# Reordering the load queue of a fused SSM and gated-MLP kernel: one x block forward, one small transpose and one row back

## The chip, the cores and the metric

The kernel runs on one core of one Trainium2 chip. The metric is the device time of one execution in microseconds. Six runs of the kernel before gave a median of 177.17 us, from 176.81 to 177.47.

## What is computed

The input x is 2048 tokens by 512 features. It is layer-normalised, and three results are added: x itself, a diagonal complex state-space layer (S5) with a skip term, and a gated MLP.

```
xn = layernorm(x)
# A: state space, P = 512 complex states
dt = exp(log_dt);  Lam_bar = exp(dt * Lambda)
Bu = xn @ B_bar.T                 # B_bar = (Lam_bar - 1) / Lambda * (B_re + i B_im)
h[t] = Lam_bar * h[t-1] + Bu[t]   # 2048 steps
yA = 2 * Re(h @ C.T) + xn * Dskip
# B: gated MLP, F = 1376
yB = (gelu(xn @ w_gate) * (xn @ w_up)) @ w_down
out = x + yA + yB
```

## The kernel before

**Tiling.** The 2048 tokens are four blocks (0 to 3) of 512 tokens; each block is four tiles of 128 tokens. `X` holds the raw tiles, `XN` the normalised ones (a ring of eight tiles), and `XNT[b]` the normalised block with features on the partitions, as TensorE needs it. A "turn" is a DMA transpose that takes one normalised tile from `XN` to `XNT` (`TR`, L736, four per block).

**Stages on TensorE (PE), in program order.** First a warm-up, then block 0's first seven gate and up column groups by another route: raw centred tiles are transposed on PE (`cent_T`, L679) and multiplied with the weights (`ks`/`GT_k` at L701, `GT_mm` at L712), and the scale of the layernorm goes into the GELU afterwards (`GT_evac`, L721 and L724). This stage needs no turn. Then `GU(0, [7, 8, 9, 10])` (L843, and L817 for the last, narrower group) does the rest of block 0's gate and up columns from `XNT[0]`; every one of its matmuls waits for all four turns of block 0. `BU(0)` and `BU(1)` (L749) multiply `XNT[0]` and `XNT[1]` by the state-space input matrices `BBT`; the first two units of `BU(1)` are halved, so that they can begin with the first two turns of block 1. After that come `GU(1)`, `BU(2)`, the down projection `DN(0)` (L884) and so on to `DN(3)`.

**VectorE (DVE), ScalarE (ACT) and GpSimd (POOL).** DVE does the layernorm statistics (`stats`, L610 and L611), the normalisation (`norms`, L629), the product of GELU and up (L724, L864), the sine tables (`tables_dve`, L597 and L599), the skip product (`SKIP`, L666) and the scan along the tokens (`CHAIN`). ACT does the GELUs and the copies out of the accumulators. POOL computes powers: the square roots of the layernorms (`root`, L617) and two exponentials of the state-space parameters (`params`, L552 for exp(log_dt), L555).

**What sets the order.** A list scheduler inside the kernel (`Sched`) places the operations of DVE, ACT and POOL by a cost model. TensorE and SyncE (SP) are in its list `INORDER`: their instructions stay in the order in which the program names them. Almost all DMAs are issued by SP, so a line's place in the program is its place in SP's queue, and an instruction of SP that waits holds up all those behind it. Up to block 1's turns SP issues, in this order:

```
x tiles of block 0 (one of them on ACT's queue), gate/up weights in pieces     L493, L484, L489
the last gate and up pieces (480 KB each), load_W                              L489
tr_par: the small transpose of log_dt, Lambda_re, Lambda_im                    L510
TR(0): four turns of block 0                                                   L736
ld_x(1): x of block 1, 512 KB                                                  L478
load_B: transposes of B_re and B_im                                            L521
        D-skip row, broadcast to 128 partitions, 128 KB                        L530
        ld_x(2): x of block 2, 512 KB                                          L478
TR(1): four turns of block 1                                                   L736
then the turns of the gated rest (L829), of block 0's hidden tiles (L730), TR(2), ...
```

The parameters of `tr_par` are read first by `params` (POOL L552, then DVE L553 and L556); the D-skip row is read first by `SKIP(0)` (L666); x of block 1 by `LN(1)` (`stats`, `root`, `norms`).

Of the kernel before, what the change touches and what calls it, by code (L numbers as in the profile page):

```python
# [352 lines left out]
def d_dve_tt2x(n): return 100.0 + 0.52 * n  # L353
# [4 lines left out]
def d_act(n, ptr=0): return 190.0 + 0.833 * n + 90.0 * ptr  # L358
# [3 lines left out]
def build(nc, ins, out):  # L362
    with ExitStack() as es:
# [113 lines left out]
        def ld_x(b):  # L477
            return S.dma(lambda e, b=b: e.dma_start(  # L478
                X_all.ap[:, 4 * b:4 * b + 4, :], x2[512 * b:512 * (b + 1), :].rearrange("(j p) d -> p j d", p=128)),
                512 * 1024, writes=X[4 * b:4 * b + 4], tag="ld_x%d" % b)  # L480
# [28 lines left out]
        def tr_par():  # L509
            S.dma(lambda e: e.dma_start_transpose(PAR.ap.rearrange("p q t -> p (q t)").unsqueeze(1), PROW16.ap), 4096,  # L510
                  reads=PROWq, writes=[PAR], tag="tr_par", issue=900.0)
# [7 lines left out]
        def load_T(bufs, nms):  # L519
            for b_, nm in zip(bufs, nms):  # L520
                S.dma(lambda e, b_=b_, nm=nm: e.dma_start_transpose(b_.ap, ins[nm]),  # L521
                      1.4 * 512 * 1024, writes=[b_], tag="tr_" + nm, issue=3000.0)

        def load_W():
            ld_w(WG, WGc, ins["B_w_gate"], 2)
            ld_w(WU, WUc, ins["B_w_up"], 2)

        def load_B():
            load_T([A.sub(BBT_all, "BBTc%d" % c, c) for c in range(2)], ("A_B_re", "A_B_im"))
            S.dma(lambda e: e.dma_start(DSKB.ap, ins["A_Dskip"].unsqueeze(0).broadcast_to([128, D])),  # L530
                  128 * 1024, writes=[DSKB], tag="ld_dsk")
            ld_x(2)

        def load_C():
            load_T(CRAW, ("A_C_re", "A_C_im"))
# [15 lines left out]
        def params():  # L551
            S.order_behind(POOL(lambda e: e.tensor_tensor(DTB.ap, EXB.ap, LDT.ap, ALU.pow), 1100, [EXB, LDT], [DTB], "exp_dt"), GATE["pow"])  # L552
            V(lambda e: e.tensor_tensor(pa(TH), DTB.ap, LIM.ap, ALU.mult), D_TINY, [DTB, LIM], [PA[TH]], "th")  # L553
            V(lambda e: e.tensor_tensor(pa(A_), DTB.ap, LRE.ap, ALU.mult), D_TINY, [DTB, LRE], [PA[A_]], "a")
            POOL(lambda e: e.tensor_tensor(pa(RRr), EXB.ap, pa(A_), ALU.pow), 1100, [EXB, PA[A_]], [PA[RRr]], "exp_a")  # L555
            V(lambda e: e.tensor_scalar(w16(0, 4), pa(TH), 1.0 / TWO_PI, None, ALU.mult), D_TINY, [PA[TH]], [W16p[0]])  # L556
            V(lambda e: e.tensor_scalar(w16(4, 8), pa(TH), 512.0 / TWO_PI, None, ALU.mult), D_TINY, [PA[TH]], [W16p[1]])
            V(lambda e: e.tensor_scalar(w16(8, 16), w16(0, 8), 0.25, None, ALU.add), D_TINY, W16p[0:2], W16p[2:4])
            V(lambda e: e.tensor_copy(KI.ap, W16.ap), D_TINY, W16p, [KI])
            V(lambda e: e.tensor_tensor(FRC.ap, W16.ap, KI.ap, ALU.subtract), D_TINY, W16p + [KI], [FRC])  # L560
# [34 lines left out]
        def tables_dve(behind):  # L595
            for s in range(KP):
                V(lambda e, s=s: e.tensor_scalar(K1s[s].ap, IOTJ.ap, W16.ap[:, s:s + 1], None, ALU.mult),  # L597
                  d_dve_ts4x(512) * 1.3, [IOTJ, W16p[0]], [K1s[s]], "k1", [GATE["evTA"]])
                V(lambda e, s=s: e.scalar_tensor_tensor(F1s[s].ap, IOTJ.ap, W16.ap[:, s:s + 1], K1s[s].ap, ALU.mult, ALU.subtract),  # L599
                  d_dve_1x(512), [IOTJ, W16p[0], K1s[s]], [F1s[s]], "f1")  # L600
            S.order_behind(V(lambda e: e.tensor_scalar(A1.ap.bitcast(I32), F1.ap.bitcast(I32), 0x7FFFFFFF, None, ALU.bitwise_and), d_dve_ts4x(2048) * 2, F1s, [A1], "a1"), behind)
# [6 lines left out]
        def stats(b, j):  # L608
            tt = 4 * b + j
            return (V(lambda e: e.bn_stats(ST[tt].ap, X[tt].ap), d_dve_1x(512), [X[tt]], [ST[tt]], "bnst"),  # L610
                    V(lambda e: e.bn_aggr(MVt[b][j].ap, ST[tt].ap), D_TINY, [ST[tt]], [MVt[b][j]], "bnag"))  # L611

        def root(b, j0, j1):
            mn, sbq, qb, rq = (cols(t, b, j0, j1) for t in (MN, SBQ, QB, RQ))
            mv = Buf("MV%d_%d_%d" % (b, j0, j1), "sb", MVt[b][j0].lo, MVt[b][j1 - 1].hi, MV[b].ap[:, j0:j1])
            op = V(lambda e: e.tensor_scalar(sbq.ap, mv.ap[:, :, 1], EPS_BF16, None, ALU.add), D_TINY, [mv], [sbq], "sbq")
            GATE["pow"] = POOL(lambda e: e.tensor_tensor(qb.ap, sbq.ap, HALF.ap[:, 0:j1 - j0], ALU.pow), 1100, [sbq, HALF], [qb], "pow")  # L617
            POOL(lambda e: e.tensor_copy(mn.ap, mv.ap[:, :, 0]), 200, [mv], [mn], "mn")
            return op, mn, qb, rq

        def recip(qb, rq):
            return V(lambda e: e.reciprocal(rq.ap, qb.ap), 150, [qb], [rq], "rq")

        def norms(b, js, mn, rq, j0):
            last = None
            for j in js:
                tt, i = 4 * b + j, j - j0
                xs = XN[tt % 8]
                last = S.order_behind(V(lambda e, tt=tt, i=i, xs=xs: e.tensor_scalar(  # L629
                    xs.ap, X[tt].ap, mn.ap[:, i:i + 1], rq.ap[:, i:i + 1], ALU.subtract, ALU.mult),  # L630
                  d_dve_ts4x(512), [X[tt], mn, rq], [xs], "ln_n"), last)
            return last

        def LN(b, js=range(4)):
            for j in js:
                stats(b, j)
            _, mn, qb, rq = root(b, js[0], js[-1] + 1)
            recip(qb, rq)
            norms(b, js, mn, rq, js[0])
# [23 lines left out]
        def SKIP(b):  # L663
            for tt in range(4 * b, 4 * b + 4):
                xs = XN[tt % 8]
                V(lambda e, tt=tt, xs=xs: e.tensor_tensor(XD[tt].ap, xs.ap, DSKB.ap, ALU.mult),  # L666
                  d_dve_tt2x(512), [xs, DSKB], [XD[tt]], "skip")
# [65 lines left out]
        def TR(b, js=range(4)):  # L733
            for j in js:
                tt = 4 * b + j
                S.dma(lambda e, b=b, j=j, tt=tt: e.dma_start_transpose(  # L736
                    XNT[b].ap[:, :, 128 * j:128 * (j + 1)], XN[tt % 8].ap),
                    1.6 * 128 * 1024, reads=[XN[tt % 8]], writes=[XTk[b][j]], tag="tr_x%d" % b, issue=1280.0)
# [212 lines left out]
                     d_dve_ts4x(512), [X[j], MVt[0][j]], [XN[j]], "sub")  # L951
        load_par()
        load_W()
        tr_par()
        S.order_behind(ACT(lambda e: e.activation(H0[3].ap[:, 0:D], X[1].ap, ACTF.Copy, scale=-1.0 / D, accum_out=NM1.ap), d_act(512) + 190,
                           [X[1]], [H0[3], NM1], "mean1"), GATE["par"])

# [58 lines left out]
        norms(0, [2], mn0, rq0, 0)  # L1016
        norms(0, [3], mn3, rq3, 3)
        TR(0, [2, 3])
        ld_x(1)
        params()  # L1020
        tables_dve(None)
        load_B()
        LN(1, [0, 1]); LN(1, [2, 3])
        TR(1)
        SKIP(0)
        GU(0, [7, 8, 9, 10])
        GATE["before_gelu"] = [tables_act([GATE["last_gelu"]])]
# [29 lines left out]
def bass_parallel_sum__ssm_conv_s5__geglu_ffn__prompt_kernel(  # L1057
    nc: bass.Bass,
    A_x: bass.AP,
    A_Lambda_re: bass.AP,  # L1060
    A_Lambda_im: bass.AP,
    A_B_re: bass.AP,
    A_B_im: bass.AP,
    A_C_re: bass.AP,
    A_C_im: bass.AP,
    A_log_dt: bass.AP,
    A_Dskip: bass.AP,
    B_x: bass.AP,
    B_w_gate: bass.AP,
    B_w_up: bass.AP,  # L1070
    B_w_down: bass.AP,
    out: bass.AP,
):
    ins = {
        "A_x": A_x, "A_Lambda_re": A_Lambda_re, "A_Lambda_im": A_Lambda_im,
        "A_B_re": A_B_re, "A_B_im": A_B_im, "A_C_re": A_C_re, "A_C_im": A_C_im,
        "A_log_dt": A_log_dt, "A_Dskip": A_Dskip,
        "B_w_gate": B_w_gate, "B_w_up": B_w_up, "B_w_down": B_w_down,
    }
    build(nc, ins, out)  # L1080
# [28 lines left out]
```

## Time and profile before

| what | before |
|---|---|
| median of 6 runs | 177.17 us (176.81 to 177.47) |
| time of the profiled execution | 176.81 us |
| its span, first to last instruction | 175.50 us |
| lies around the span | 1.31 us |
| PE busy | 172.1 us, 98% of the span |
| DVE busy | 159.7 us, 91% |
| ACT busy | 95.0 us, 54% |
| POOL busy | 9.8 us, 6% |
| granted TensorE clock | 1.000 in every slice |
| bytes moved by DMA | 14.36 MB, 82 GB/s on the mean |

PE is the busy engine, and the chain that ended last runs almost only through it, so a microsecond in which PE stands still is a microsecond of the kernel. The mean rate of the DMA is low, but the loads are bunched: in the first 40 us most slices of the span show the 16 DMA engines nine tenths busy or more. What matters about a DMA here is when it lands, not how many bytes there are in all.

### The profile page before, as it was taken

How to read it: one execution, taken by the hardware profiler on the slowest of the kernel's cores; microseconds unless marked ns; L12 is line 12 of the kernel's file. 1: busy time of each engine (PE TensorE's matmuls, PEld its weight loads, DVE VectorE, ACT ScalarE, POOL GpSimd, SP SyncE). 2: the span in 40 equal slices, each digit the busy share in tenths (PEclk: the TensorE clock that was granted, in tenths of full speed). 3: DMA queues.
4: the chain of work that ended last, by engine and by line, in shares of the span. 5: the costliest groups of instructions: out<-in, count | busy, mean ns of one | idle time of the engine just before them, and what ended most of it. 6: DMA issues, size and time to landing. Idle time of an engine off the chain costs nothing.

```text
span 175.5 us, 2485 instructions
## 1 busy us (share of the span) xinstructions
PE 172.1 (98%) x866; PEld 84.0 (48%) x881; DVE 159.7 (91%) x278; ACT 95.0 (54%) x187; POOL 9.8 (6%) x24
## 2 busy tenths in 40 slices
PE   8999999999999999999999999999999999999995
PEld 3545464645544444444644444444464444444454
DVE  6886999997999999789999999999999999999941
ACT  5474768899876898365666792000657970000000
POOL 3132040202000000001000000000000000000000
PEclk9999999999999999999999999999999999999999
DMA  4899999595999000002034000002001000000312
GB/s 145 257 314 195 246 156 204 90 141 103 175 242 318 8 0 2 0 30 71 23 68 83 0 0 0 4 0 90 30 0 30 4 0 0 0 0 0 120 64 62
DMA packets 32420, 14.36 MB, mean 82 GB/s; under 512 B 23736, under 2 KB 32408, under 8 KB 32408
## 3 DMA queue, kind: packets, MB, share of 16 engines
q1 hardware_dynamic: 32240, 14.07, 35.9%
q8 instruction: 7, 0.11, 0.3%
q10 hardware_dynamic: 168, 0.13, 0.2%
q14 instruction: 5, 0.04, 0.1%
HBM read 6.46 MB, written 2.10 MB: 49 GB/s over the span
## 4 chain that ended last, share of the span: by engine, by line
PE 98%; issue 1%; DVE 0%
PE PS L884 37%; PE PS L843 32%; PE PS L749 16%; PE PS L712 4%; PE PS L701 3%; PE PS L817 3%; PE PS L933 2%; PE PS L679 1%; PE PS L940 0%; DVE arena L902 0%
## 5 line engine op out<-in xcount | busy, mean ns | idle before, releaser
L884 PE MATMUL PS<-arena 128*128 128x512 bf16 (+3 forms) x317 | 65.9, 366 | 0.3
L843 PE MATMUL PS<-arena 128*128 128x512 bf16 x257 | 57.1, 379 | 0.4
L884 PEld LDWEIGHTS PS<-arena 128*128 128x128 bf16 (+1 forms) x323 | 30.8, 98 | 35.2
L843 PEld LDWEIGHTS PS<-arena 128*128 128x128 bf16 x264 | 25.8, 98 | 30.3
L787 DVE TENSOR_TENSOR_SCAN arena<-arena 128x512 bf16<-128x512 f32 x32 | 38.8, 1252 | 0.0
L858 ACT ACTIVATE arena<-PS 128x512 bf16<-128x512 f32 x33 | 19.8, 599 | 24.6 <-DVE arena L902 16.7
L749 PE MATMUL PS<-arena 128*128 128x512 bf16 (+1 forms) x134 | 28.0, 366 | 0.1
L862 ACT ACTIVATE arena<-PS 128x512 bf16<-128x512 f32 x33 | 19.8, 601 | 4.7 <-PE PS L843 4.7
L876 ACT ACTIVATE PS<-arena 128x512 f32<-128x512 bf16 (+2 forms) x17 | 9.6, 581 | 19.7 <-DVE arena L902 19.0
L749 PEld LDWEIGHTS PS<-arena 128*128 128x128 bf16 x136 | 13.3, 98 | 14.1
L758 ACT ACTIVATE arena<-PS 128x512 bf16<-128x512 f32 x32 | 17.6, 593 | 1.6 <-PE PS L749 1.5
L902 DVE TENSOR_TENSOR arena<-PS,arena 128x512 bf16<-128x512 f32 (+2 forms) x17 | 10.8, 651 | 6.3 <-PE PS L884 6.3
L864 DVE TENSOR_TENSOR arena<-arena 128x512 bf16<-128x512 bf16 x33 | 13.2, 417 | 2.2 <-ACT arena L862 2.0
L776 DVE TENSOR_TENSOR arena<-arena 128x4096 bf16<-128x4096 bf16 (+1 forms) x5 | 9.2, 1858 | 0.3 <-ACT arena L606 0.3
L799 DVE TENSOR_TENSOR arena<-arena 128x4096 bf16<-128x4096 bf16 x4 | 9.2, 2289 | 0.1
L774 DVE TENSOR_TENSOR arena<-arena 128x4096 bf16<-128x4096 bf16 (+1 forms) x5 | 9.2, 1857 | 0.0
L800 DVE TENSOR_TENSOR arena<-arena 128x4096 bf16<-128x4096 bf16 x4 | 9.1, 2285 | 0.0
L610 DVE BATCH_NORM_STATS2 arena<-arena 128x6 f32<-128x512 bf16 x12 | 7.7, 678 | 0.6 <-DMA arena<-in_A_x_dram 0.6
L721 ACT ACTIVATE arena<-PS,arena 128x256 bf16<-128x256 f32 (+1 forms) x16 | 6.1, 447 | 2.7 <-DVE arena L556 1.8
L712 PE MATMUL PS<-arena 128*128 128x512 bf16 (+1 forms) x40 | 7.1, 336 | 0.0
L724 DVE SCALAR_TENSOR_TENSOR arena<-PS,arena 128x256 bf16<-128x256 f32 (+1 forms) x16 | 6.2, 443 | 0.3 <-PE PS L701 0.3
L701 PE MATMUL PS<-arena 128*128 128x512 bf16 (+1 forms) x28 | 6.2, 364 | 0.0
(95 smaller groups left out, 123.6 us busy)
## 6 DMA issues: line engine op xcount, KB each, us to landing
out_dram<-arena SPq DMA_DIRECT2D x15, 128.0 KB, 1.7
arena<-in_A_x_dram SPq DMA_DIRECT2D x3, 512.0 KB, 5.5
arena<-in_B_w_down_dram SPq DMA_DIRECT2D x1, 1280.0 KB, 7.3
arena<-in_B_w_gate_dram SPq DMA_DIRECT2D x4, 128.0 KB, 3.0
arena<-in_B_w_up_dram SPq DMA_DIRECT2D x4, 128.0 KB, 3.1
arena<-in_B_w_gate_dram SPq DMA_DIRECT2D x1, 480.0 KB, 6.9
arena<-in_B_w_up_dram SPq DMA_DIRECT2D x1, 480.0 KB, 7.8
arena<-arena SPq DMA_TRANSPOSE x25, 3.1
```

Of the source, the lines that this page charges most:

```text
L701: PE(lambda e: e.matmul(dst, XCd(j, k), WGU[:, ws[0]:ws[-1] + 1, k, f0:f1], start=first, stop=k == KD - 1, skip_group_check=True), d_pe([w ...
L712: ins_ = e.matmul(dst, XCd(j, k), WGU[:, :, k, f0:f1], start=(k == 0), stop=(k == KD - 1))
L749: ins_ = e.matmul(PS[bank][:, 128 * j0:128 * j1], BBT[c][dk].ap[:, 128 * s:128 * (s + 1)], XNT[b].ap[:, dk, 128 * j0:128 * j1], start=(dk ...
L758: GATE["evBu"] = ACT(lambda e, bank=bank, k3=k3, s=s, c=c: e.activation(SSc[k3][s][c].ap, PS[bank][:, :], ACTF.Copy), d_act(512), [BANK[ba ...
L787: V(lambda e, g=g, rb=rb, init=init: e.tensor_tensor_scan(g.ap, rb, g.ap, init, ALU.mult, ALU.add), d_dve_scan(512), [g, PA[RRr]] + ([CARc ...
L843: ins_ = e.matmul(PS[bank][0:m, c0:c1], W.ap[:, dk, 128 * ft:128 * ft + m], XNT[b].ap[:, dk, c0:c1], start=(dk == 0), stop=(dk == KD - 1))
L858: GATE["last_gelu"] = ACT(lambda e, bg=bg, kk=kk, m=m: e.activation(GG[kk].ap[0:m, :], PS[bg][0:m, :], ACTF.Gelu_apprx_tanh), d_act(512), ...
L862: ACT(lambda e, bu=bu, kk=kk, m=m: e.activation(UPB[kk].ap[0:m, :], PS[bu][0:m, :], ACTF.Copy), d_act(512), [BANK[bu]], [UPB[kk]], "evU")
L864: V(lambda e, kk=kk, m=m, ft=ft, k2=k2: e.tensor_tensor(HTt[k2][ft].ap[0:m, :], GG[kk].ap[0:m, :], UPB[kk].ap[0:m, :], ALU.mult), d_dve_tt ...
L876: ACT(lambda e: e.activation(PS[bank][:, c0:c1], X[tt].ap[:, c0:c1], ACTF.Copy), d_act(c1 - c0), [X[tt]], [BANK[bank]], "seed")
L884: ins_ = e.matmul(PS[bank][:, c0:c1], l_[:, 128 * j:128 * (j + 1)], r_[:, c0:c1], start=False, stop=last and n == len(ops) - 1, skip_group ...
L902: V(lambda e: e.tensor_tensor(OUTB[ko].ap[:, c0:c1], PS[bank][:, c0:c1], XD[tt].ap[:, c0:c1], ALU.add), d_dve_1x(c1 - c0), [BANK[bank], XD ...
```

## The change

Three DMAs of SP's queue change place. x of block 1 is issued straight after the last weight pieces, where the parameter transpose stood. The parameter transpose comes behind the four turns of block 0, where x of block 1 stood. The D-skip row leaves its place between the B transposes and x of block 2 and is issued behind the four turns of block 1.

```diff
         def load_B():
             load_T([A.sub(BBT_all, "BBTc%d" % c, c) for c in range(2)], ("A_B_re", "A_B_im"))
+
+        def load_skip():
             S.dma(lambda e: e.dma_start(DSKB.ap, ins["A_Dskip"].unsqueeze(0).broadcast_to([128, D])),
                   128 * 1024, writes=[DSKB], tag="ld_dsk")
-            ld_x(2)
...
         load_par()
         load_W()
-        tr_par()
+        ld_x(1)
...
         TR(0, [2, 3])
-        ld_x(1)
+        tr_par()
         params()
         tables_dve(None)
         load_B()
+        ld_x(2)
         LN(1, [0, 1]); LN(1, [2, 3])
         TR(1)
+        load_skip()
         SKIP(0)
```

No instruction is added or removed. The built programs show what the scheduler makes of it. PE and POOL keep their order. On ACT two GELUs of the L721 group change places. On DVE two statistics of block 1 (L610) move forward between the last products L724: the first stands where the parameter product L553 stood, ahead of seven of these products, the second ahead of four. L553 and its scaling L556 move back, behind the statistics of block 1. Of the four L597 operations of the sine tables, three stood between the products and one behind block 1's statistics; now one stands behind the statistics and three behind block 1's normalisation.

## Prediction

> **What bounds the kernel.** I read the chain that ended last first, then its pieces around the changed DMAs.
>
> ```profile
> PE 98%; issue 1%; DVE 0%
> ...
> 17.99 0.08 issue
> 18.07 5.12 PE PS L843 x23
> 23.19 1.32 PE PS L817 x16
> 24.51 2.16 PE PS L749 x10
> ```
>
> The columns are start, length, what. TensorE (PE) makes up the whole path. The busy time by stretch of the span shows how little else there is:
>
> ```profile
> 10.90:160.00 149.10, 148.33 (x733) 71.92 (x746) 142.12 (x236) 89.53 (x175) 6.19 (x9) 1.00 0.35 73
> ```
>
> After the length come the busy times of PE, weight load, DVE, ACT and POOL. From 10.90 to 160 us PE stands still for 149.10 - 148.33 = 0.77 us in all. The stage before 10.90 us reads nothing that the change moves, and the last 15.5 us are the final down projection. So no reordering here can win more than 0.77 us, and each microsecond by which PE is made to wait is added in full: no later hole takes it up.
>
> Next SP's queue, from the timeline (start, length, instruction):
>
> ```profile
> 7.52 0.51 SPq L489 DMA_DIRECT2D arena<-in_B_w_up_dram  x1
> 8.15 1.82 SPq L510 DMA_TRANSPOSE arena<-arena  x1
> 10.15 5.30 SPq L736 DMA_TRANSPOSE arena<-arena  x4
> 15.50 0.59 SPq L478 DMA_DIRECT2D arena<-in_A_x_dram  x1
> 16.13 3.02 SPq L521 DMA_TRANSPOSE arena<-in_A_B_re_dram  x1
> ```
>
> The four turns of block 0 start at 10.15, 11.42, 12.74 and 14.19. From issue to landing the DMA view gives, for the last up piece, for the fourth turn alone, and for x of block 1:
>
> ```profile
> arena<-in_B_w_up_dram SPq DMA_DIRECT2D x1, 480.0 KB, 7.8
> ```
>
> ```profile
> arena<-arena SPq DMA_TRANSPOSE x1, 3.1
> ```
>
> ```profile
> arena<-in_A_x_dram SPq DMA_DIRECT2D x1, 512.0 KB, 3.8
> ```
>
> So the up piece lands at 7.52 + 7.8 = 15.3, the fourth turn at 14.19 + 3.1 = 17.3, x of block 1 at 15.50 + 3.8 = 19.3. The first three turns take 5.7, 4.9 and 4.0 and land at 15.85, 16.3 and 16.7. PE ends L712 at 17.99 and goes on with L843, which needs all four turns: **they have 0.7 us in hand**. This is the number on which the case turns.
>
> Last, what the DMA engines move: packets under 512 B are the transposes, larger ones the copies. The stretches are 13 to 14, 14 to 14.75, 14.75 to 15, 15 to 15.5 and 17.5 to 18.5 us:
>
> ```profile
> DMA packets 628, 0.32 MB, mean 319 GB/s; under 512 B 387, under 2 KB 628, under 8 KB 628
> DMA packets 184, 0.07 MB, mean 92 GB/s; under 512 B 149, under 2 KB 184, under 8 KB 184
> DMA packets 49, 0.01 MB, mean 38 GB/s; under 512 B 49, under 2 KB 49, under 8 KB 49
> DMA packets 531, 0.13 MB, mean 260 GB/s; under 512 B 531, under 2 KB 531, under 8 KB 531
> DMA packets 362, 0.37 MB, mean 371 GB/s; under 512 B 0, under 2 KB 362, under 8 KB 362
> ```
>
> The first turn's packets mix with the tail of the weights from 13 us on: each DMA engine goes to the turn when its share of the weights is done. Some engines are late; the rate sinks to 38 GB/s, although turns two and three were issued long ago. Then at 15.0 all run again, with small packets only: the second turn has waited until the first was through. From 15.0 to 16.7 the other three go through, and a landing shows some 0.7 us after the last packet.
>
> **x of block 1 ahead of the turns.** One DMA, 0.59 us of SP, in the place of one of 1.82 us. SP is free by about 8.7 instead of 9.97; the first turn still starts at 10.15, because it waits for the first normalisation (L629, from 9.71, three in 1.06 us). So issue neither gains nor loses. The data do: 512 KB now stand between the weights and the turns. Their price: by the 371 GB/s of this same transfer 0.524 MB / 0.371 = 1.4 us; by the landings of the two last weight pieces (13.9 and 15.3 for 480 KB, so 1.45 us), scaled to 512 KB, 1.55 us; by the landings of the last middle piece and the gate piece (11.9 and 13.9) 2.0 x 512/480 = 2.1 us. From below: between 14.0 and 15.0 the engines moved about 0.08 MB, where 0.31 MB would fit at 307 GB/s (the mean from 8 to 14 us). If x filled that hole, 0.23 MB of it would be free, and 0.29 MB, 0.7 to 0.9 us, would remain. I take 1.5 us, the hole not filled, because the late engines set the end of the first turn, and their share of x comes on top of their late weights.
>
> A page speaks against this. The Trainium skill, "DMA: Bandwidth & Descriptors", section "Queues, rings and completion order", says that each DMA engine takes its descriptors in ring order, that data descriptors carry no barrier, and that completion is not first-in first-out per issuer. By that alone an engine done with x would run turns one to four without regard to the others. The start of the second turn on all engines at 15.0 shows otherwise; by the page the stall below would come to some 0.4 us.
>
> **The parameter transpose behind the turns.** In its old place it costs the turns almost nothing: the up piece lands at 15.3, the transpose 8.15 + 7.5 = 15.65, the first turn 15.85. Taking it out of the way is worth 0 to 0.2 us; I take 0.1. The four turns thus land 1.5 - 0.1 = 1.4 us later, the last at 18.7, which is 0.7 us behind the end of L712. With some 0.1 us from landing to the first matmul (PE shows 0.08 "issue" there now) **PE stands still for 0.8 us**; from the ends, 0.7 - 0.7 = 0 us and 2.1 - 0.7 + 0.1 = 1.5 us.
>
> Its new place delays its readers. Issued at 15.5, it lands behind the fourth turn, about 19.2. POOL's exp(log_dt), 15.78 now for 1.02 us, then runs from 19.3 to 20.3, ahead of the square roots of block 1 (23.33 now), which are queued behind it. DVE's first reader is now behind block 1's statistics:
>
> ```profile
> 16.90 0.16 DVE L553 TENSOR_TENSOR arena<-arena 128x4 f32<-128x4 bf16 x1 [1.69 <-POOL arena L552]
> ```
>
> DVE waited 1.69 us there, until 16.90. In the changed order it waits in the same gap for x of block 1, which lands at about 15.3 + 1.5 = 16.8: one wait for another. Behind this wait stand seven products L724 that empty accumulators. The first of them, which frees the bank of the first L843 matmul, ends one statistic (0.62) and one product (0.4) later, at 17.9; PE with its stall comes at 18.8. The last ends some 3.6 us after the landing, at 20.4 against 20.2 now, for banks asked for at 22 and later. Nothing to add: the stall covers it. DVE then does the other statistics at 20.7 instead of 21.9, the square roots start at about 22.1, the parameters are there since 20.3. Block 1 is normalised by 25.1 instead of 26.4.
>
> On SP, `tr_par` moves the B transposes back: they start at about 17.3 instead of 16.13, and B_im at 20.4 instead of 19.19. B_im now lands 5.3 us after its start, so about 25.7; B_re took 6.7 us, at most 24.0. BU(0) begins on B_re at 24.4 + 0.8 and on B_im four units (3.5 us) later. Free, with 1.2 us in hand; without that cover a later B_re would cost PE one for one.
>
> **The D-skip row behind block 1's turns.** It moves slowly: 24 to 25.5 us runs at 50 to 115 GB/s, so x of block 2 and the turns behind it gain about 1 us, which pays for the later B transposes. Turns of block 1 are issued from about 24.1 instead of 24.87 and land 0.5 to 1 us earlier than now (29.2 to 31.6). BU(1) asks for them at 31.2 and 32.1, so nobody on PE sees the gain. The row itself is issued near 29.4 (0.58 us), in front of the turns L829 and L730, where SP waits for DVE until 31.13 anyway. It lands 3 to 4.7 us later, at 32.4 to 34.1; SKIP(0) (34.21 now) is its first reader. Zero, with little in hand; 0.5 us late would hold only DVE, and DVE's result is wanted by PE after 70 us.
>
> **Sum.** On the profiled execution 176.81 + 0.8 = 177.6 us. The six runs have their median 0.36 us above that execution, and I lay the stall on the median: 177.17 + 0.8 = 177.97, say 178.0 us.
>
> **Rivals.** *Hidden (0.15).* x fills the hole of 14 to 15 us: the turns land 0.7 us later, just as L712 ends. 177.0 to 177.3 us. For it: at 38 GB/s most of the rate lies unused. Against it: the end of a turn is set by the latest engine.
>
> *Faster (0.12).* In the profiled execution the turns of block 1 land 0.1 to 2 us ahead of need. If in the usual run they come late and PE waits at BU(1), this is where its 0.36 us go, and turns 0.5 to 1 us earlier give them back: 177.17 - 0.36 = 176.8 us. It decides only if the turns of block 0 also land before 18.0. Against it: PE shows no wait there.
>
> *Slower by more (part of the 0.73).* x costs 2.1 us: PE waits 1.5 us, 178.7 us.
>
> That the change does not do what it says can be ruled out for the order; that the DMA engines take x out of turn is the hidden case.
>
> **Numbers.** Slower has 0.73, of which the forecast (a stall of 0.4 to 1.5 us, 177.6 to 178.7) nearly all. About 0.2%, 0.35 us, is what a measurement can tell from no change: within it 0.15, faster 0.12. The range runs from 176.9, into the faster case and over the hidden one, to 178.7. Within the forecast alone it is 177.6 to 178.6.
>
> **What would show it.** Right: after L712 PE stops for 0.5 to 1.2 us before L843, released by the turns (landing 18.5 to 19), the L478 transfer lands at 16.5 to 17.2, DVE waits for it at L611, and later stages are only shifted. Wrong: L843 starts by 18.2, or the turns land before 18.0; or PE shows new waits at L749, from B_re or from an accumulator that DVE frees late.

## The result, and the profile after

The changed kernel takes 177.73 us on the median of 22 runs, the kernel before 177.17 us (48 runs): 0.56 us more. The ratio, here and below formed over the runs and not from the two medians, is 1.0033, with a 95% interval from 1.0023 to 1.0044. A few executions of the changed kernels had a lower granted clock (0.99); no time, ratio or profile here uses them, so e5_x1_only below stands without a profile. The change is slower, by a third of a per cent. Its profiled execution takes 177.38 us, with a span of 176.0 us.

The changed program has one line more ahead of its stages, so L844 here is L843 of the kernel before; in the experiments the numbers shift by up to six.

The page's chain that ended last is no longer PE alone. A DMA of x stands in it, by way of a DVE statistic that waits for x; below it turns out that PE did not wait for this statistic:

```profile
PE 88%; DMA 5%; SPq 4%; issue 1%; DVE 1%; DVEq 0%
```

SP's queue after (timeline: start, length, instruction):

```profile
7.54 0.55 SPq L489 DMA_DIRECT2D arena<-in_B_w_up_dram  x1
8.13 1.68 SPq L478 DMA_DIRECT2D arena<-in_A_x_dram  x1
9.95 6.36 SPq L737 DMA_TRANSPOSE arena<-arena  x4
16.44 1.14 SPq L510 DMA_TRANSPOSE arena<-arena  x1
```

The DMA view gives the time from issue to landing of the x transfer and of the fourth turn (issued at 15.05):

```profile
arena<-in_A_x_dram SPq DMA_DIRECT2D x1, 512.0 KB, 8.1
```

```profile
arena<-arena SPq DMA_TRANSPOSE x1, 3.1
```

So x of block 1 lands at 16.2, the fourth turn at 15.05 + 3.1 = 18.15; before, 14.19 + 3.1 = 17.29. The view gives the time to landing to one decimal, so landings are known to 0.05 us, here and below. The packets in the stretches 15.75 to 16 and 16 to 16.25 us show the same step as before at 15.0, one microsecond later:

```profile
DMA packets 49, 0.01 MB, mean 41 GB/s; under 512 B 49, under 2 KB 49, under 8 KB 49
DMA packets 276, 0.07 MB, mean 277 GB/s; under 512 B 276, under 2 KB 276, under 8 KB 276
```

And this is what PE shows at the group that needs the turns, in its chain of work and in its waits:

```profile
18.44 0.04 issue
18.49 5.12 PE PS L844 x23
23.61 1.32 PE PS L818 x16
```

```profile
PE PS L844 <- DVE arena L611: 0.3, 1, 0.3
```

The group starts later than the 18.07 of before, and the profile puts the wait down to a DVE statistic, not to a turn. This needs care. The group has 24 matmuls, and only 23 are recorded (x23): the record of the first is missing. The next group starts at 23.45 in the timeline, and 24 matmuls at 0.216 us take 5.18 us, so the first one ran from 23.45 - 5.18 = 18.27. That is some 0.1 us behind the landing of the fourth turn and ahead of the end of the statistic named (18.44). The same correction puts the first matmul of the kernel before at 23.03 - 5.18 = 17.85, not 18.07.

DVE exchanged one wait for another, as forecast:

```profile
16.24 0.69 DVE L611 BATCH_NORM_STATS2 arena<-arena 128x6 f32<-128x512 bf16 x1 [0.77 <-DMA arena<-in_A_x_dram]
```

### The profile page after: what moved, and what is told of

Read it like the earlier page. It is cut to its first block, busy times and chain, and to the rows that moved or that the text cites. A ratio compares the mean times of both kernels' runs of the same rounds, so it can differ in the third digit from the quotient of the medians.

```text
span 176.0 us, 2484 instructions
## 1 busy us (share of the span) xinstructions
PE 172.0 (98%) x866; PEld 83.7 (48%) x881; DVE 160.0 (91%) x278; ACT 95.4 (54%) x187; POOL 9.9 (6%) x24
## 4 chain that ended last, share of the span: by engine, by line
PE 88%; DMA 5%; SPq 4%; issue 1%; DVE 1%; DVEq 0%
PE PS L885 37%; PE PS L844 32%; PE PS L750 16%; DMA arena<-in_A_x_dram 5%; PE PS L818 3%; SPq L484 2%; SPq L489 1%; SPq L493 1%; DVE arena L725 1%; DVE arena L611 0%; DVE arena L903 0%; DVEq L337 0%
## 5 line engine op out<-in xcount | busy, mean ns | idle before, releaser
L844 PE MATMUL PS<-arena 128*128 128x512 bf16 x257 | 57.1, 379 | 0.6 <-DVE arena L611 0.3
L844 PEld LDWEIGHTS PS<-arena 128*128 128x128 bf16 x264 | 25.7, 98 | 30.5 <-issue 0.3
L713 PE MATMUL PS<-arena 128*128 128x512 bf16 (+1 forms) x40 | 7.1, 336 | 0.0
```

What stands on the lines that cost most here:

```text
L844: ins_ = e.matmul(PS[bank][0:m, c0:c1], W.ap[:, dk, 128 * ft:128 * ft + m], XNT[b].ap[:, dk, c0:c1], start=(dk == 0), stop=(dk == KD - 1))
```

## Experiments

The theory: x of block 1 ahead of the turns makes the turns land late, and PE waits for the fourth. Rivals: DVE frees an accumulator late (the profile names it); the late parameters or the late D-skip row cost the time; or the early weights do, by chance. Ratios are against the kernel before on the same chip.

**The changed kernel again (e1_again).** No edit.

> The changed kernel itself once more, for a second profile. Theory (the turns of block 0 land late behind x of block 1, and PE waits for the fourth one): first L844 matmul 0.2 to 0.4 us behind the landing of the fourth turn, at 18.3 to 18.9 us against 18.07 before; time 0.4 to 0.8 us above the kernel before. Rival (chance of the early weights: the first profile after has 0.25 us of PE idle at 6 us too): the idle at 6 us is seen again and is about half of the loss.

Measured: 177.87 us against 177.37, ratio 1.0037 (1.0015 to 1.0060). The profiled execution is a long one of 179.90 us. All 24 matmuls are recorded this time, and the wait has another name:

```profile
PE PS L844 <- DMA arena<-arena: 2.3, 1, 2.3
```

The fourth turn lands at 20.66, the first matmul is at 20.75, 0.1 us behind it (0.2 to 0.4 expected). Both are far beyond the 18.9 expected: the last weight piece landed a microsecond later than in the first profile after (15.8 against 14.8), and there was a gap between two turns, to which the last section comes back. The idle at 6 us is not there; e6_x1_half, below, has 0.3 us of the same kind in a profile of 177.03 us, without a loss.

**x of block 1 back behind the turns (e2_x1_back).**

```diff
 load_W()
-ld_x(1)
...
 TR(0, [2, 3])
+ld_x(1)
 tr_par()
```

> x of block 1 goes back behind the four turns; the parameter transpose (behind x) and the D-skip row stay where the change put them. Theory: the fourth turn lands at 17.3 us or earlier, the first L844 matmul follows L713 without a wait, at about 18.0, and the time is that of the kernel before within 0.2 us (177.0 to 177.4). Rival (the late parameters or the late D-skip row cost the time): still 0.4 us or more slower than before.

Measured: 177.26 us against 177.37, ratio 0.9991 (0.9979 to 1.0004). The loss is gone. The fourth turn lands at 16.93, and in the chain the group follows L713 without a piece between:

```profile
18.40 5.18 PE PS L844 x24
```

**Statistics of block 1 behind the products on DVE (e3_dve_late).** The changed load queue is kept.

```diff
 for j in js:
-    stats(b, j)
+    op, _ = stats(b, j)
+    if b == 1:
+        S.order_behind(op, GATE["hm"])      # the last product of GT_evac
```

The two products of `coefs` that read only parameters are ordered behind it as well, so that they do not slip forward.

> The load queue of the changed kernel, but on DVE the statistics of block 1 are ordered behind all products L725, so that DVE no longer stands waiting for x of block 1 with products behind it. Theory (turns): no gain, PE starts the group after L713 as late as in the changed kernel, 18.3 to 18.9 us; time 177.5 to 178.0. Rival (the chain after names a DVE statistic as the releaser: PE waits for an accumulator that DVE frees late): PE starts by 18.1 and the time goes back to 177.1 to 177.4.

Measured: 177.63 us against 177.37, ratio 1.0021 (0.9999 to 1.0044). The times alone leave it open whether a part of the loss came back. In the profile the wait is still there: PE waits 0.9 us for a transpose that SP issued at 15.97, though DVE now does all the products ahead of block 1's statistics.

```profile
15.97 3.09 DMA arena<-arena
19.05 0.14 issue
19.19 5.34 PE PS L846 x24
```

The group starts at 19.19, later than the 18.9 expected, because the turn lands at 19.07. The rival on DVE asked for a start by 18.1 and falls as the cause of this wait.

**Twice the dose (e4_x1x2).**

```diff
 load_W()
 ld_x(1)
+ld_x(2)
...
 load_B()
-ld_x(2)
```

> Twice the dose: x of block 2 (another 512 KB) is issued right behind x of block 1, also ahead of the turns of block 0; the rest as in the changed kernel. Theory: the fourth turn lands 1.4 us later than in the changed kernel, at about 19.6, and PE adds this in full: first L844 matmul near 19.9, time 1.2 to 1.6 us above the changed kernel, 178.9 to 179.4. Rival (the loss does not come from bytes ahead of the turns): within 0.4 us of the changed kernel.

Measured: 179.32 us, ratio 1.0119 (1.0087 to 1.0151), 1.45 us above e1_again. The fourth turn lands at 19.97, the group starts at 20.07. x of block 1 lands at 16.6 and x of block 2 at 18.0: some 1.4 us for another 512 KB.

```profile
PE PS L849 <- DMA arena<-arena: 1.9, 1, 1.9
```

**Half the dose (e6_x1_half).** `ld_xp(1, 0, 2)` loads the first two tiles of block 1, `ld_xp(1, 2, 4)` the others.

```diff
 load_W()
-ld_x(1)
+ld_xp(1, 0, 2)
...
 TR(0, [2, 3])
+ld_xp(1, 2, 4)
 tr_par()
```

> Half the dose: the changed kernel with only the first two tiles of block 1 (256 KB) ahead of the turns, the other two behind them. Theory (bytes ahead of the turns, 1.4 us for 512 KB, of which 0.7 us were in hand): the fourth turn lands 0.7 us earlier than in the changed kernel, at about 17.5 to 17.8, and PE waits 0 to 0.1 us: time within 0.2 us of before. Rival (a fixed cost of any copy between weights and turns): as slow as the changed kernel, 177.6 to 177.9.

Measured: 177.23 us against 177.34, ratio 0.9991 (0.9972 to 1.0011). The half lands some 0.75 us behind the weights (14.9 and 15.6), the fourth turn at 17.59. PE has no wait at this group:

```profile
18.19 0.05 issue
18.24 5.13 PE PS L849 x23
```

A copy ahead of the turns is thus not harmful by itself: the bytes count, and only those beyond what is in hand.

**One move alone.** x ahead (e5_x1_only), the D-skip row back (e7_skip_only), the parameter transpose back (e8_par_only), each on the kernel before.

```diff
 load_W()
+ld_x(1)             # e5 only
-tr_par()            # e8 only
...
 TR(0, [2, 3])
+tr_par()            # e8 only
-ld_x(1)             # e5 only
...
 TR(1)
+load_skip()         # e7 only, taken out of load_B
```

> The kernel before with one move alone: x of block 1 ahead of the parameter transpose and the turns; the parameter transpose stays ahead of the turns, the D-skip row stays between the B transposes and x of block 2. Theory (x ahead of the turns is the whole loss): 0.4 to 0.8 us slower than before; if the small transpose costs the turns 0.1 us as I took it, 0.5 to 0.9. Rival (the three moves share the loss): under 0.3 us slower.

> The kernel before with one move alone: the D-skip row behind the turns of block 1. Theory: nothing on PE, time of before within 0.2 us; the turns of block 1 land 0.5 to 1 us earlier than before (29.2 for the first). Rival (block 1's turns come late in the usual run, and PE waits there): 0.2 to 0.4 us faster than before.

> The kernel before with one move alone: the parameter transpose behind the turns of block 0, ahead of x of block 1 (which stays behind the turns). Theory: the turns land up to 0.2 us earlier, PE does not wait, time of before within 0.2 us. Rival (the late parameters cost): 0.3 us or more slower.

Measured against 177.34: e5_x1_only 177.79, ratio 1.0042 (1.0017 to 1.0068; four of its eleven runs, from 178.57 to 179.35, lift it); e7_skip_only 177.13, ratio 0.9991 (0.9974 to 1.0008); e8_par_only 177.43, ratio 1.0009 (0.9991 to 1.0027). x alone makes the whole loss. The D-skip row behind the turns let x of block 2 land at 26.2 and the first turn of block 1 at 27.0 instead of 29.2 (0.5 to 1 us was expected; the fourth came at 31.6 as before), and brought no measurable gain: PE does not wait for block 1's turns.

**More profiles (e9_before_look, e10_after_look, e11_after_look, e12_x1_only_look).** One further profile each, no edit against the kernels they are named after.

> A second profile of the kernel before. Theory (the time of all these kernels is the start of the L843 group plus a constant): the turns land by 17.4 us, PE does not wait for them, and the time less the start of the L817 group behind it is 153.8 us as in the first profile. Rival (the spread of the kernel before comes from later stages): that difference moves by over 0.3 us.

> Another profile of the changed kernel, to see where the fourth turn usually lands: 18.15 and 20.66 us so far, 19.07 with the products ahead on DVE. Theory: between 18.1 and 19.2, time 159.0 to 159.3 us above the first matmul of the L844 group, unless a large packet of an instruction queue falls among the turns; then about 1.5 us later. Rival (the packet is chance and unrelated): a late turn without such a packet.

> The same once more: fourth turn between 18.1 and 19.2 us without a packet of an instruction queue among the turns, near 20.5 with one; the time follows the start of the L844 group.

> Another profile of the kernel before with x of block 1 alone moved ahead (the parameter transpose still ahead of the turns). Theory: the fourth turn as in the changed kernel or up to 0.2 us later, 18.2 to 19.4 us, and PE waits for it; no other wait. Rival: the parameter transpose ahead of the turns costs over 0.3 us there.

The profiles together, in us. "PE ready" is the start of L712 plus the 6.94 us that its 40 matmuls and the change to the next group take where nothing waits. "First matmul" is that of the L843 group, worked out from the start of the L817 group, less 5.18.

| run | 4th turn lands | PE ready | first matmul | time | time less first matmul |
|---|---|---|---|---|---|
| before | 17.29 | 17.84 | 17.85 | 176.81 | 158.96 |
| e9, before | 17.17 | 18.46 | 18.44 | 177.41 | 158.97 |
| e2, x back | 16.93 | 18.25 | 18.24 | 177.32 | 159.08 |
| e6, half of x | 17.59 | 18.04 | 18.03 | 177.03 | 159.00 |
| e7, skip only | 16.95 | 18.01 | 18.00 | 176.97 | 158.97 |
| e8, parameters only | 16.60 | 18.20 | 18.19 | 177.15 | 158.96 |
| after | 18.15 | 18.09 | 18.27 | 177.38 | 159.11 |
| e10, after | 18.76 | 18.38 | 18.89 | 177.94 | 159.05 |
| e11, after | 19.74 | 18.24 | 19.91 | 179.10 | 159.19 |
| e1, after | 20.66 | 18.15 | 20.75 | 179.90 | 159.15 |
| e3, DVE late | 19.07 | 18.15 | 19.19 | 178.26 | 159.07 |
| e12, x only | 18.26 | 18.21 | 18.35 | 177.40 | 159.05 |
| e4, x twice | 19.97 | 18.02 | 20.07 | 179.32 | 159.25 |

The first matmul comes at the later of two times: when PE is ready, or 0.1 to 0.2 us behind the fourth turn. The rest of the kernel takes 158.96 to 159.25 us whatever was moved. Nearly all of the difference between these thirteen executions is the start of this one group: from the start of the L817 group behind it to the end of the last matmul all thirteen take 150.62 us, and the remaining 0.3 us lies behind that. e11's turn came at 19.74, earlier than the 20.5 that was expected with a large packet (the last section explains it), and its first matmul follows the turn as in the others. Where the record of the first matmul is missing and PE waits (x23), the wait is put down to DVE; where it is there (e1, e3, e4), to the DMA.

The fourth turn in its turn follows the weights. The last up piece lands between 14.7 and 15.8 us in these profiles. The fourth turn comes 1.9 to 2.0 us behind it where no x lies between, 2.7 to 2.8 with half of x, 3.3 to 3.5 with x (after, e10, e3, e12) and 4.9 with two. Only e1 and e11, at 4.8 with one x, fall out of this order. So x costs the turns some 1.4 us each time, and on top of that the landing of the turns moves with that of the weights.

## Why the prediction was right, and where it was off

**Right: what bounds, and where the wait appears.** Slower was given 0.73, with the fourth turn of block 0 behind x as the one cause. The wait came at this group and nowhere later; the hidden and the faster rival both fell, the second with e7_skip_only. (By the prediction's own figures block 1's last turn was 0.5 us ahead of need, 31.6 against 32.1, not 0.1.) Of the signs it named, the first profile after shows none in full: the wait is 0.18 us (0.5 to 1.2 named), the fourth turn at 18.15 (18.5 to 19), x at 16.2 (16.5 to 17.2). e10 shows all three: 0.51, 18.76 and 16.8.

**Right: the price of x.** 1.5 us was taken for 512 KB between weights and turns. Landing after landing, x follows the last up piece by 1.4 to 1.5 us in the seven profiles that have it there, between the 1.4 by the transfer's own rate and the 1.55 by the weight pieces. The lower bound, x filling the hole of late DMA engines, did not happen: after as before the rate sinks to 41 GB/s until the first turn is through. The Trainium skill ("DMA: Bandwidth & Descriptors", section "Queues, rings and completion order") speaks of ring order without a barrier; in the trace the second turn again starts only when the first is done, at 16.0. That the stall by the page, 0.4 us, for which the prediction shows no working, is nearer to what was measured than mine is no merit of that mechanism.

**Right: the parameter transpose costs the turns little.** From the landing of the copy ahead to that of the first turn it is some 0.6 us with the transpose between them, some 0.5 without: about 0.1 us, as taken.

**Off: the sum, 0.8 us against 0.56.** The step that failed is "I lay the stall on the median". The profiled execution of before was one in which PE was ready early, at 17.84; in the other profiles without a wait it is ready between 18.01 and 18.46, because the first 11 us vary. A late PE and a late turn do not add up: the later one counts. So the 0.36 us by which the median lay above that execution had to be taken out of the stall, not added to it. In the profile after, 0.25 us of the shift of 0.42 us is a later start of L713 (11.15 against 10.90), and only 0.18 us is waiting. The turns came early there as well, because the last up piece landed at 14.8 instead of 15.3. In hand I also read 0.7 us, from the modelled end of the last matmul; from the first matmul of the next group, less 0.1 us, it was 17.75 - 17.29 = 0.46 us in that execution, and more in the usual one (1.2 us in e9). The two slips pull opposite ways. With both put right, an estimate from the rows of the first execution is 176.81 + 1.4 - 0.46 = 177.75 us, against 177.73 measured; that 177.97 came as near as it did is in part luck.

**Off: SP's issue.** The x transfer was given 0.59 us of SP and took 1.68, and the first two turns took 1.89 and 1.80 instead of some 1.25. The fourth turn was issued at 15.05 instead of 14.19. It cost nothing here, since from 16.0 to 17.5 the DMA engines had turns to move without a gap. Of the landings behind it: parameters 18.64 (19.2 forecast), B_im 25.2 (25.7), turns of block 1 at 28.3 to 30.1 (0.5 to 1 us earlier forecast, 0.7 to 1.6 measured), D-skip row 32.6 (32.4 to 34.1). None is waited for by PE, as forecast.

## What to carry to other kernels

A transfer that nobody needs yet still costs when it is put into a queue ahead of one that the bound engine is about to need: count the bytes ahead of the needed transfer, price them by the spacing of landings in that queue, and compare with the time in hand. Take the time in hand from more than one execution, and take the later of two arrivals; a stall is not added to a median that already holds the other arrival's lateness. Before believing a named releaser, count the records of the group: with the first one missing, the wait gets the name of whatever ended last ahead of the second.

## What was not expected of the hardware

**A large packet of an instruction queue among the turns.** In e1_again the first two turns land at 17.78 and 18.30, the third at 20.25. SP issued it at 14.85, and its data ran with the others; but from 18.5 to 20.5 us only 12 to 77 packets pass per half microsecond, where some 500 passed before. The stretches are 17.5 to 18 and 19 to 19.5 us:

```profile
DMA packets 487, 0.12 MB, mean 239 GB/s; under 512 B 487, under 2 KB 487, under 8 KB 487
DMA packets 12, 0.00 MB, mean 5 GB/s; under 512 B 12, under 2 KB 12, under 8 KB 12
```

In the half microsecond from 18.0 the DMA view shows, in the list of queues (packets, MB, share):

```profile
q8 instruction: 1, 0.02, 14.1%
```

e11 is alike: such a packet from 17.0 to 17.5, the second turn at 17.43, the third at 19.33. In the eleven other profiles, where no such packet fell before the third turn was in, it follows the second by 0.4 to 0.5 us. A later transfer shows the same: the parameter transpose lands 2.2 us behind its issue in the profile after, and 4.1 in e10 (packet between 18.5 and 19). No run took the packet away, so that it is the cause is argued, not shown. It would explain why runs of 179 us and more occur with x ahead of the turns (2 of the 22 of the result, 1 of 12 in e1_again), while the longest of the 112 runs of the kernel before that stand beside the runs here is 178.47: in the kernel before the turns are in by 17.3 us, and the first such packet behind the start fell at 17.0 us or later in every profile.

**SP's time to issue a copy is not a constant of the copy.** A 512 KB copy takes SP 0.59 us at 15.5 us in the kernel before, 1.68 at 8.1 us in the changed one, right behind the weights; the two copies of e4_x1x2 take 2.60 together, and the half copy of e6_x1_half, at the same place, 1.79. So it is the place and not the size. That the work still queued at that place is the reason is argued, not shown.
